# A linear attention and gated MLP kernel: the spatial products of one more batch in quarters, and a new written order

## The chip, the cores and the metric

One Trainium2 chip, one NeuronCore of it. The metric is the device time of one execution in microseconds (us), the median of the runs shown. The engines are named as in the profile: PE (TensorE) multiplies matrices, PEld is its loading of weights, DVE (VectorE), ACT (ScalarE) and POOL (GpSimd) work element by element, SP (SyncE) issues the DMAs. PE writes into PSUM, the rest lies in SBUF.

## What is computed

```python
f = 1.0 / (1.0 + np.exp(-f_logit))                  # q, k, v, f_logit: [4, 8, 768, 48]
for t in range(S):                                  # forgetting linear attention
    state = f[:, :, t, :, None] * state + np.einsum('bhd,bhe->bhde', k[:, :, t], v[:, :, t])
    y[:, :, t] = np.einsum('bhd,bhde->bhe', q[:, :, t], state)
x = y.transpose(0, 2, 1, 3).reshape(4, 768, 384)
h = np.maximum(x @ w_in, 0.0)                       # w_in [384, 1024]
u, v = (h[..., :d_ff // 2], h[..., d_ff // 2:])     # 512 columns each
v_n = (v - mu) / np.sqrt(var + 1e-06)               # layer norm of each row of v
v_s = np.einsum('ts,bsd->btd', w_spatial, v_n) + b_spatial[None, :, None]   # w_spatial [768, 768]
out = (u * v_s) @ w_out                             # w_out [512, 384]
```

Products are made in three passes: each operand is split into a high part (fp32r) and the low rest, and high x high, high x low and low x high are summed in PSUM.

## The kernel before

**A written order.** `PLAN` (line 46) is a list of steps; `run` calls `step_<name>` with the numbers behind the colon. Within `tc.manual_schedule()` each engine does its instructions in the order of that list, so an instruction that waits holds up all that stands behind it on its engine. `BESIDES` (line 114) names the steps that go to POOL in place of their usual engine. Buffers are `Slots`: `take` gives the buffer that has been free longest, `done` gives it back after the stated number of uses, and so the order of the plan also says whose buffer each step inherits.

**Attention.** 24 units (4 batches x 6 blocks of 128 rows, number n), each a chain of small steps: c, e, z, h, g, k, q and fm prepare forget factors, keys and queries (DVE, ACT, POOL; fm copies the last factors into `ends`), X are the scores on PE (L384), w, m, kv, YS, Yq, r0 to r2 the rest, ys copies the result, xt transposes it on PE into an `mm` bank, and xh (ACT) and xl (DVE) take it out of there as high and low part of `xT`.

**The MLP**, b = batch, th = half of the rows: V:b,u (nine products of 512 columns, L493) with vr, bs, na, nb, nc, vn (layer norm) and vh, vl (high and low part, buffers `vns`, six pairs); U:b,th,c (nine of 384, L584) with ur; S:b,th,c, the spatial product (18 of 384, L598) with sg (DVE, adds the bias); sm multiplies with u (POOL, L614); sh, sl split; O:b,th,tt (twelve of 384, L629; the last three in a part Oa and a part O) with oc (copy) and od (store). PSUM is `mm`, four single banks of 512 columns for V, U, S, O and the transposes, and `bp`, two pairs of them for the attention.

**Batch 3 in quarters.** Batches 0 to 2 make v_s of eight S steps a batch. Batch 3 takes the 2 x 2 blocks of w_spatial and v_n and makes seven block products in place of eight (Strassen's way, in Winograd's form). The block sums of w_spatial come from the steps LR:i (a load on SP of two of its row blocks into a buffer of `raws`), ra:i (four subtractions that depend on each other), th, tl, rh, rl (split into `low_b`, `out_b`, `cross_b`; rl:i gives the raw buffer back). Those of v_n, some of them in the vr buffers themselves, come from vd, dh, dl, sa (three instructions that depend on each other), zh, zl, yh, yl. The products are P:k,m (L779), k = 1 to 7 and m = 0, 1, nine of 384 columns each; xa to xg (DVE, L793) add them out of PSUM. "more" and "fast" hand over buffers of finished stages to `raws`, `vrs`, `uTs` and `gts`, "fast" after the last attention unit.

**The flag.** marks, check and load count the forget factors that underflow; hint (L839) lets PE load the flag and announces the jump at L885 to its sequencer, 45 products ahead of the end. The jump's target, which does everything again in another way, isn't entered with these inputs.

Of the kernel before, what the change touches and what calls it, by code (L numbers as in the profile page):

```python
# [40 lines left out]
LAST_C = 1  # L41
SUMMED = 6
# [61 lines left out]
    zh:2 xc:0 P:4,0 xc:1 P:4,1 zh:0 xb:1 zl:0 sa:1 O:2,1,2 zh:1 yh:2 zl:1 O:2,1,0 xb:0 sm:3,0,0 zl:2 check load P:6,1
    yh:1 oc:2,1,2 od:2,1,2 yh:0 sm:3,0,1 yl:1 ur:3,1,0 xd:1 sh:3,0,1 P:6,0 O:2,1,1 xd:0 sh:3,0,0 yl:2 yl:0 xe:1 xe:0
    P:5,0 sm:3,0,2 sm:3,0,3 sh:3,0,3 U:3,1,3 xf:0 P:3,0 sm:3,1,2 sh:3,0,2 sl:3,0,2 sl:3,0,1 sl:3,0,3 sh:3,1,2 oc:2,1,1
    od:2,1,1 oc:2,1,0 od:2,1,0 sl:3,0,0 P:5,1 ur:3,1,3 xg:0 sm:3,1,0 O:3,0,1 oc:3,0,1 od:3,0,1 xf:1 sm:3,1,3 O:3,0,0
    oc:3,0,0 od:3,0,0 O:3,0,2 oc:3,0,2 od:3,0,2 P:3,1 hint U:3,1,1 sh:3,1,0 sl:3,1,0 sh:3,1,3 ur:3,1,1 sl:3,1,2 xg:1
    sl:3,1,3 sm:3,1,1 Oa:3,1,0 sh:3,1,1 Oa:3,1,2 sl:3,1,1 O:3,1,0 oc:3,1,0 od:3,1,0 O:3,1,2 Oa:3,1,1 oc:3,1,2 od:3,1,2
    O:3,1,1 oc:3,1,1 od:3,1,1  # L110
# [4 lines left out]
    c:1 c:3 r2:0 c:5 r2:2 c:6 r2:3 c:7 c:9 c:8 r2:6 c:10 r2:7 r2:8 c:13 r2:10 r2:12 c:16 c:17 r2:14 c:19 r2:16 c:20  # L115
    r2:18 c:22 r2:19 r2:21 q:23 ra:1 r2:22 vd:1 vn:3,5
# [26 lines left out]
def tile_kernel(ctx, tc, fkq, fn, vv, w_cv, w_spT, b_sp, out):  # L143
# [524 lines left out]
    def step_fast():  # L668
# [9 lines left out]
        for slots, more in ((uTs, tiles(pool, "uT_fast", 2, [P, TH])), (vrs, tiles(pool, "vr_fast", 2, [P, G])), (gts, tiles(pool, "gt_fast", 2, [P, TH]))):  # L678
# [8 lines left out]
    def low_b(i):  # L687
        return [x[:, i] for x in xTs.of("t1")]
# [35 lines left out]
    def step_vd(i):  # L724
        x = vrs.of((B - 1, i))
        other("vd", i, nc.vector).tensor_tensor(x[:, right], x[:, left], x[:, right], op=ALU.subtract)

    def step_dh(i):
        nc.scalar.copy(vns.of((B - 1, i))[0][:, right], vrs.of((B - 1, i))[:, right])

    def step_dl(i):
        (hi, lo), x = vns.of((B - 1, i)), vrs.of((B - 1, i))
        nc.vector.tensor_tensor(lo[:, right], x[:, right], hi[:, right].bitcast(F32), op=ALU.subtract)

    def step_sa(i):

        x, y = vrs.of((B - 1, i)), vrs.of((B - 1, HK + i))
        eng = other("sa", i, nc.vector)
# [4 lines left out]
    def step_zh(i):  # L743
        high_of(vns.take(("z", i), 4), vrs.of((B - 1, HK + i)))

    def step_zl(i):
        low_of(vns.of(("z", i)), vrs.of((B - 1, HK + i)))
        vrs.done((B - 1, HK + i))

    def low_sum(i):  # L750
# [258 lines left out]
```

## Time and profile before

| | |
|---|---|
| median of the 3 runs shown | 348.38 us (348.37 to 349.01) |
| the profiled execution | 347.48 us |
| its span | 345.9 us |
| DMA | 38.48 MB |

The span runs from the first to the last instruction or transfer in the trace; the rest of an execution lies around it. A row of the trace has a start and a duration; since the engines are pipelined, an instruction may start a little ahead of the former's end. In a group of waits, "A <- B" reads: A's engine sat idle until B ended.

### The profile page before, as it was taken

How to read it: one execution, taken by the hardware profiler on the slowest of the kernel's cores; microseconds unless marked ns; L12 is line 12 of the kernel's file. 1: busy time of each engine (PE TensorE's matmuls, PEld its weight loads, DVE VectorE, ACT ScalarE, POOL GpSimd, SP SyncE). 2: the span in 40 equal slices, each digit the busy share in tenths (PEclk: the TensorE clock that was granted, in tenths of full speed). 3: DMA queues.
4: the chain of work that ended last, by engine and by line, in shares of the span. 5: the costliest groups of instructions: out<-in, count | busy, mean ns of one | idle time of the engine just before them, and what ended most of it. 6: DMA issues, size and time to landing. Idle time of an engine off the chain costs nothing.

```text
span 345.9 us, 10531 instructions
## 1 busy us (share of the span) xinstructions
PE 334.6 (97%) x4571; PEld 308.7 (89%) x4571; DVE 230.8 (67%) x445; ACT 181.0 (52%) x373; POOL 88.0 (25%) x103
## 2 busy tenths in 40 slices
PE   7888999999999999999999999999999999999995
PEld 5666788998999989899999889999999999999995
DVE  2898999985989898762755585662221796975420
ACT  7577898956457467732274356652222635522232
POOL 3215505302320061311603051007111125002500
PEclk9999999999999999999999999999999999999999
DMA  7989665151454221350330206210230031000112
GB/s 240 341 262 355 226 219 215 18 195 55 176 156 171 94 82 64 132 161 16 101 115 24 93 25 229 72 49 0 52 134 2 0 114 48 0 0 25 45 71 75
DMA packets 15508, 38.48 MB, mean 111 GB/s; under 512 B 1504, under 2 KB 9952, under 8 KB 15456
## 3 DMA queue, kind: packets, MB, share of 16 engines
q1 hardware_dynamic: 15456, 37.75, 32.0%
q8 instruction: 37, 0.61, 0.8%
q14 instruction: 15, 0.12, 0.1%
HBM read 33.03 MB, written 4.72 MB: 109 GB/s over the span
## 4 chain that ended last, share of the span: by engine, by line
PE 85%; DVE 6%; DMA 3%; ACT 2%; issue 2%; POOL 0%; SPq 0%; DVEq 0%; ACTq 0%
PE mm L598 22%; PE mm L629 14%; PE mm L584 13%; PE mm L493 13%; PE bp L779 6%; PE bp L384 5%; PE bp L436 3%; PE bp L448 3%; PE bp L408 2%; PE mm L460 2%; DMA fkq<-fn 2%; DMA late<-w_spT 1%; DVE fkq L356 1%; PE mm L339 1%; PE mm L779 1%
## 5 line engine op out<-in xcount | busy, mean ns | idle before, releaser
L614 POOL TENSOR_TENSOR uT<-gt,uT 128x384 f32<-128x384 f32 x24 | 26.8, 1126 | 53.9 <-DVE gt L607 23.8
L324 POOL TENSOR_SCALAR fkq<-fkq 112x512 f32<-112x512 f32 (+1 forms) x14 | 21.8, 1555 | 43.6 <-DMA fkq<-fkq 17.7
L427 POOL TENSOR_TENSOR sA<-sA,F 112x192 f32<-112x192 f32 x14 | 9.7, 691 | 80.1 <-DVE sA L422 79.7
L598 PE MATMUL mm<-w_sph,vnh 128*128 128x384 f32 x144 | 29.9, 342 | 0.0
L598 PE MATMUL mm<-w_sph,vnl 128*128 128x384 f32 x144 | 29.2, 338 | 0.0
L598 PE MATMUL mm<-w_spl,vnh 128*128 128x384 f32 x144 | 29.2, 338 | 0.0
L646 ACT COPY osb<-mm 128x384 f32<-128x384 f32 x24 | 11.1, 481 | 28.7 <-PE mm L629 27.0
L598 PEld LDWEIGHTS mm<-w_spl,vnh 128*128 128x128 f32 x144 | 25.6, 188 | 0.0
L598 PEld LDWEIGHTS mm<-w_sph,vnl 128*128 128x128 f32 x144 | 25.6, 188 | 0.0
L598 PEld LDWEIGHTS mm<-w_sph,vnh 128*128 128x128 f32 x144 | 25.2, 188 | 0.4
L607 DVE TENSOR_TENSOR gt<-mm,b_bc 128x384 f32<-128x384 f32 x23 | 12.7, 551 | 18.9 <-PE mm L598 18.8
L384 PE MATMUL bp<-q,fkq 48*64 48x112 f32 x768 | 23.9, 261 | 1.1 <-issue 0.4
L475 DVE TENSOR_TENSOR xTl<-mm,xTh 128x384 fp32r<-128x384 f32 x24 | 13.3, 552 | 16.0 <-ACT xTh L470 15.9
L356 DVE SCALAR_TENSOR_TENSOR fkq<-fkq 112x512 f32<-112x512 f32 x24 | 18.2, 757 | 8.5 <-ACT fkq L350 4.7
L334 DVE TENSOR_TENSOR_SCAN fkq<-runs,fkq 112x512 f32<-112x512 f32 x18 | 22.9, 1277 | 0.7 <-ACT fkq L329 0.6
L584 PE MATMUL mm<-xTh,w_inh 128*128 128x384 f32 x96 | 22.8, 346 | 0.0
L384 PEld LDWEIGHTS bp<-q,fkq 48*64 48x64 f32 x768 | 19.0, 133 | 3.9 <-issue 1.7
L584 PE MATMUL mm<-xTl,w_inh 128*128 128x384 f32 x96 | 22.1, 338 | 0.0
L584 PE MATMUL mm<-xTh,w_inl 128*128 128x384 f32 x96 | 22.1, 338 | 0.0
L493 PE MATMUL mm<-w_inh,xTh 128*128 128x512 f32 x72 | 22.0, 413 | 0.0
L629 PE MATMUL mm<-w_outh,gh 128*128 128x384 f32 x96 | 21.8, 344 | 0.0
L622 DVE TENSOR_TENSOR gl<-uT,gh 128x384 fp32r<-128x384 f32 x27 | 15.1, 570 | 9.2 <-ACT gh L618 9.2
(210 smaller groups left out, 823.0 us busy)
## 6 DMA issues: line engine op xcount, KB each, us to landing
fkq<-fkq SPq DMA_DIRECT2D x18, 768.0 KB, 4.8
val<-vv SPq DMA_DIRECT2D x24, 192.0 KB, 4.5
out<-osb SPq DMA_DIRECT2D x24, 192.0 KB, 2.0
words<-w_cv SPq DMA_DIRECT2D x4, 768.0 KB, 7.9
fkq<-fkq SPq DMA_DIRECT2D x6, 512.0 KB, 5.5
late<-w_cv SPq DMA_DIRECT2D x2, 768.0 KB, 5.3
late<-w_spT SPq DMA_DIRECT2D x2, 768.0 KB, 6.1
fkq<-fn SPq DMA_DIRECT2D x6, 192.0 KB, 3.7
```

Of the source, the lines that this page charges most:

```text
L324: other("c", n, nc.vector).tensor_scalar(f, f, -LOGIT_MOST, None, op0=ALU.max)
L334: return nc.vector.tensor_tensor_scan(f[0:DP], runs, f[0:DP], 0.0, op0=ALU.mult, op1=ALU.add)
L356: other("k", n, nc.vector).scalar_tensor_tensor(k, f, 1.0 / F_LEAST, k, op0=ALU.min, op1=ALU.mult)
L384: nc.tensor.matmul(sc[to, e, cs], k[dr, at:at + C], qs[n % 2][dr, j, chunk], start=True, stop=True)
L475: nc.vector.tensor_tensor(x[1], mm.of(("xt", n))[:, 0:HD].rearrange("p (c t) -> p c t", c=KX), x[0].bitcast(F32), op=ALU.subtract)
L493: nc.tensor.matmul(acc, xs[:, c, ut * P:(ut + 1) * P], ws[:, c, G:FF], start=i == 0, stop=i == 3 * KX - 1)
L584: nc.tensor.matmul(acc[:, 0:TH], ws[:, kx, cs], xs[:, kx, :], start=i == 0, stop=i == 3 * KX - 1)
L598: nc.tensor.matmul(acc[:, 0:TH], vns.of((b, ks))[va][:, cs], w_sp_s[wb][:, ks, th * TH:(th + 1) * TH], start=i == 0, stop=i == 3 * KS - 1,)
L614: nc.gpsimd.tensor_tensor(uT, gts.of((b, th, c)), uT, op=ALU.mult)
L622: nc.vector.tensor_tensor(lo, uTs.of((b, th, c)), hi.bitcast(F32), op=ALU.subtract)
L629: nc.tensor.matmul(acc[:, 0:DM], gs.of((b, th, c))[ga][:, ts], w_out_s[wb][:, c, :], start=c == cs[0] != LAST_C and ga == wb == 0, stop=c ...
L779: nc.tensor.matmul(acc, vns.of(user(i))[va][:, cs], b(i)[wb], start=n == 0 and k in (1, 2, 7), stop=n == 3 * HK - 1, skip_group_check=True)
```

## The change

Batch 2 is made in quarters as well (`FAST = 2, 3`), so its eight S steps go and 14 P steps, P:2,k,m, come with the steps around them: vd, dh, dl, sa, zh, zl, yh, yl and xa to xg take the batch as a first number. Batch 2 needs the upper blocks of v_n again after their low parts are made; a new step rc (two additions, high + low) makes the values anew from the parts where the buffer was needed in between.

The whole plan from sl:0,0,0 on is in a new order. The loads of w_spatial's blocks come as LR:0, 2, 1, ra is on DVE for all of them, and the raw buffers go LR:0 <- "more", LR:2 <- "fast", LR:1 <- rl:0. `low_b` lies in a part of `w_sp` that nothing reads any more, and not in an `xT` buffer. "fast" hands over four vr and one uT in place of two and two. POOL gets sa, vd, rc, vn and q steps by the new `BESIDES`, and loses ra:1. hint stands 138 products ahead of the end.

```diff
+FAST = 2, 3
 PLAN:
-    V:3,4 bs:3,2 ur:2,1,1 th:1 tl:1 xh:23 xl:23 V:3,5 bs:3,1 ur:2,1,2 marks na:3,0 bs:3,3 vr:3,4 S:2,1,2 LR:2 sl:2,0,3
-    rh:1 vr:3,5 bs:3,4 S:2,1,3 od:1,1,1 rl:1 od:1,1,0 LR:0 bs:3,5 ra:2 nb:3,0 sg:2,1,2 sh:2,0,1 sl:2,0,1 na:3,1 nb:3,1
...
+    sl:1,1,3 r2:22 kv:23 r0:23 Yq:22 ys:22 V:3,1 vn:2,4 vl:2,3 r1:23 Yq:23 ur:2,0,3 rc:2,0 xh:21 xl:21 vh:2,4 xt:22
+    xh:22 ys:23 P:2,1,0 vl:2,4 ur:2,0,0 vr:3,1 xt:23 dh:2,2 tl:0 xh:23 fm:23 fast rh:0 LR:2 V:3,2 ra:2 vr:3,2 rl:0
+    U:2,1,1 fm:22 O:1,1,0 od:1,0,1 dl:2,2 rc:2,2 ur:2,1,1 xa:2,0 xl:23 P:2,2,0 sa:2,2 rh:2 P:2,1,1 th:2 oc:1,1,0
+    od:1,0,2 od:0,1,0 LR:1 O:1,1,1 tl:2 V:3,5 ra:1 rl:2 sa:2,0 xa:2,1 rh:1 marks th:1 tl:1 xl:22 rl:1 oc:1,1,1 od:1,1,1
+    O:1,1,2 rc:2,1 P:2,7,0 sa:2,1 P:2,7,1 bs:3,1 zh:2,2 zh:2,0 xc:2,0 P:2,4,0 zh:2,1 zl:2,2 P:2,2,1 oc:1,1,2 od:1,1,2
...
+    ur:2,1,0 O:2,0,0 U:3,0,0 vl:3,0 oc:2,0,0 od:2,0,0 vd:3,2 P:3,1,1 vd:3,0 vn:3,4 sm:2,1,3 sm:2,1,1 vn:3,3 ur:3,0,1
+    dh:3,1 vh:3,3 xg:2,0 vl:3,5 P:3,1,0 O:2,0,2 dl:3,1 vl:3,3 sm:2,1,0 xa:3,1 xa:3,0 dh:3,0 dh:3,2 vh:3,4 vl:3,4 sa:3,1
+    O:2,0,1 dl:3,0 dl:3,2 P:3,7,1 xc:3,1 oc:2,0,2 od:2,0,2 sm:2,1,2 sh:2,1,2 sh:2,1,3 P:3,7,0 sa:3,0 sl:2,1,2 sh:2,1,1
...
 BESIDES:
-    c:1 c:3 r2:0 c:5 r2:2 c:6 r2:3 c:7 c:9 c:8 r2:6 c:10 r2:7 r2:8 c:13 r2:10 r2:12 c:16 c:17 r2:14 c:19 r2:16 c:20
-    r2:18 c:22 r2:19 r2:21 q:23 ra:1 r2:22 vd:1 vn:3,5
+    c:1 c:3 r2:0 c:5 r2:2 c:6 r2:3 c:7 c:9 c:8 r2:6 c:10 r2:7 r2:8 c:13 r2:10 r2:12 c:16 r2:13 c:17 vn:1,5 q:16 vn:1,4
+    r2:15 q:17 c:18 c:19 r2:16 q:19 c:20 c:22 r2:19 vn:2,1 vd:2,1 vd:2,0 q:21 r2:20 r2:21 vd:2,2 vn:2,4 sa:2,2 sa:2,0
+    rc:2,1 sa:2,1 vn:3,0 vd:3,0 vn:3,3 sa:3,0 sa:3,2
...
 step_vh:
-        if b == B - 1:
+        if b in FAST:
             n = 2 * P if u < HK else G
-            return nc.scalar.copy(vns.take((b, u), 4)[0][:, 0:n], vrs.of((b, u))[:, 0:n])
+            return nc.scalar.copy(vns.take((b, u), 5 if b == FAST[0] else 4)[0][:, 0:n], vrs.of((b, u))[:, 0:n])
...
 low_b:
-        return [x[:, i] for x in xTs.of("t1")]
+        return [w[:, i, TH:S] for w in w_sp_s]
...
+    def step_rc(b, i):
+        for u in (i, HK + i):
+            hi, lo = (x.bitcast(F32) for x in vns.of((b, u)))
+            other("rc", (b, i), nc.vector).tensor_tensor(vrs.take((b, u)), hi, lo, op=ALU.add)
+            vns.done((b, u))
```

## Rows read from the trace of the kernel before

**Rows 1.** The page, part 1: engine, busy us, share of the span, instructions.

```profile
PE 334.6 (97%) x4571; PEld 308.7 (89%) x4571; DVE 230.8 (67%) x445; ACT 181.0 (52%) x373; POOL 88.0 (25%) x103
```

**Rows 2.** Busy time by stretch: length, PE, PEld, DVE, ACT, POOL, PEclk, DMA.

```profile
120.00:342.40 222.40, 221.86 (x2445) 210.63 (x2443) 130.62 (x265) 97.05 (x207) 55.54 (x56) 1.00 0.20 65
```

**Rows 3.** PE's waits from 120 us on: us in total, times, longest.

```profile
PE bp L779 <- DVE gt L793: 0.3, 1, 0.3
PE bp L384 <- DVE fkq L356: 0.2, 1, 0.2
```

**Rows 4.** The chain of work: start, us, engine, line; products of a step.

```profile
169.59 2.09 PE mm L629 x12
...
229.66 3.17 PE mm L598 x18
...
243.18 2.09 PE mm L493 x9
...
332.90 1.58 PE bp L779 x9
```

**Rows 5.** PE and ACT in order of time: start, us, what.

```profile
270.59 0.94 PE L493 MATMUL mm<-w_inh,xTh 128*128 128x512 f32 x3
270.87 0.48 ACT L470 CAST xTh<-mm 128x384 fp32r<-128x384 f32 x1
...
273.46 0.50 ACT L700 CAST t3h<-late 128x384 fp32r<-128x384 f32 x1
273.86 0.83 ACT L700 CAST qt2h<-late 128x768 fp32r<-128x768 f32 x1
```

**Rows 6.** DVE in order of time, in stretches without POOL.

```profile
279.08 0.56 DVE L697 TENSOR_TENSOR raw_fast<-raw_fast 128x384 f32<-128x384 f32 x1
...
295.66 0.54 DVE L703 TENSOR_TENSOR t3l<-raw_fast,t3h 128x384 fp32r<-128x384 f32 x1
296.13 0.94 DVE L703 TENSOR_TENSOR qt2l<-raw_fast,qt2h 128x768 fp32r<-128x768 f32 x1
```

**Rows 7.** POOL in order of time: a vd, a q and a vn step.

```profile
235.93 1.28 POOL L360 TENSOR_TENSOR q<-fkq,F 112x512 f32<-112x512 f32 x1
...
282.79 0.98 POOL L726 TENSOR_TENSOR vr<-vr 128x256 f32<-128x256 f32 x1 [1.34 <-DVE vr L552]
...
287.60 2.62 POOL L552 TENSOR_SCALAR vr_fast<-vr_fast,mv,rs 128x512 f32<-128x512 f32 x1 [3.83 <-issue]
```

**Rows 8.** DVE and POOL in order of time, where both are at work.

```profile
35.06 0.96 DVE L260 SCALAR_TENSOR_TENSOR words<-words 128x768 int32<-128x768 int32 x1
36.04 0.51 POOL L427 TENSOR_TENSOR sA<-sA,F 112x192 f32<-112x192 f32 x1
36.06 1.31 DVE L261 SCALAR_TENSOR_TENSOR words<-words 128x768 int32<-128x768 int32 x1
...
41.58 1.61 POOL L369 COPY ends<-F 112x4 f32<-112x4 f32 x1
...
124.22 0.99 DVE L356 SCALAR_TENSOR_TENSOR fkq<-fkq 112x512 f32<-112x512 f32 x1
...
315.54 0.95 DVE L703 TENSOR_TENSOR vnl<-vr,vnh 128x256 fp32r<-128x256 f32 x1 [1.01 <-ACT vnh L700]
...
322.56 1.01 POOL L614 TENSOR_TENSOR uT<-gt,uT 128x384 f32<-128x384 f32 x1 [0.56 <-DVE gt L793]
323.06 0.92 DVE L622 TENSOR_TENSOR gl<-uT,gh 128x384 fp32r<-128x384 f32 x1 [0.59 <-ACT gh L618]
```

**Rows 9.** Instructions of the flag's load and of the jump on PE's queue.

```profile
L839 PEldq TENSOR_LOAD <-bad x1: 490/490/490, 331.2 to 331.2; - x1
...
L885 PEldq COMPARE_BRANCH  x1: 393/393/393, 339.1 to 339.1; - x1
```

**Rows 10.** DMA issues, 274 to 285 and 245 to 256 us: KB, us to landing.

```profile
late<-w_spT SPq DMA_DIRECT2D x1, 768.0 KB, 4.9
...
raw_fast<-w_spT SPq DMA_DIRECT2D x1, 768.0 KB, 5.6
```

More of the change, by code (lines that the diff above doesn't have):

```diff
@@ L104 @@
[L104 to L108, printed above, removed]
@@ new lines @@
+    yl:3,0 yh:3,1 zl:3,2 zl:3,1 zl:3,0 load P:3,6,0 sm:3,0,0 O:2,1,2 O:2,1,1 yl:3,2 yl:3,1 xd:3,0 P:3,5,0 sl:3,0,1 hint
+    P:3,6,1 xd:3,1 O:2,1,0 ur:3,0,3 oc:2,1,2 od:2,1,2 xe:3,0 xf:3,0 sm:3,0,2 xe:3,1 sh:3,0,0 sm:3,0,3 oc:2,1,1 od:2,1,1
+    sl:3,0,0 P:3,3,0 xg:3,0 sh:3,0,2 P:3,5,1 sh:3,0,3 sl:3,0,3 sm:3,1,0 sl:3,0,2 U:3,1,2 O:3,0,1 oc:3,0,1 od:3,0,1
+    O:3,0,2 ur:3,1,2 oc:3,0,2 od:3,0,2 sm:3,1,2 xf:3,1 oc:2,1,0 od:2,1,0 sm:3,1,3 sh:3,1,2 O:3,0,0 sh:3,1,3 oc:3,0,0
+    od:3,0,0 sl:3,1,3 P:3,3,1 sh:3,1,0 sl:3,1,0 xg:3,1 U:3,1,1 ur:3,1,1 sl:3,1,2 Oa:3,1,1 sm:3,1,1 Oa:3,1,2 sh:3,1,1
@@ L676, in pair @@
             return [tuple(pool.tile([P, width], F32R, name=f"{name}{k}{i}") for k in "hl") for i in range(HK)]
-        for slots, more in ((uTs, tiles(pool, "uT_fast", 2, [P, TH])), (vrs, tiles(pool, "vr_fast", 2, [P, G])), (gts, tiles(pool, "gt_fast", 2, [P, TH]))):
+        for slots, more in ((uTs, tiles(pool, "uT_fast", 1, [P, TH])), (vrs, tiles(pool, "vr_fast", 4, [P, G])), (gts, tiles(pool, "gt_fast", 2, [P, TH]))):
             slots.free.extend(more)
@@ L705, in step_th @@
     def step_th(i):
-        if "t1" not in xTs.held:
-            xTs.take("t1", 2)
         high_of(low_b(i), raws.of(i)[:, 0, 0:TH])
@@ L722, in tile_kernel, with step_vd, right_of, step_dh @@
     left, right = slice(0, W2), slice(W2, G)
[L724 to L738, printed above, removed]
+    def step_vd(b, i):
+        x = vrs.of((b, i))
+        other("vd", (b, i), nc.vector).tensor_tensor(x[:, right], x[:, left], x[:, right], op=ALU.subtract)
+    def right_of(user):
+        return [x[:, right] for x in vns.of(user)]
+    def step_dh(b, i):
+        high_of(right_of((b, i)), vrs.of((b, i))[:, right])
+    def step_dl(b, i):
+        low_of(right_of((b, i)), vrs.of((b, i))[:, right])
+        if b == FAST[0]:
+            vrs.done((b, i))
+    def step_rc(b, i):
[3 more added lines that the diff above has]
+            vns.done((b, u))
+    def step_sa(b, i):
+        x, y = vrs.of((b, i)), vrs.of((b, HK + i))
+        eng = other("sa", (b, i), nc.vector)
         eng.tensor_tensor(y[:, right], y[:, right], x[:, right], op=ALU.subtract)
@@ L741, in step_sa, with step_zh, step_zl, low_sum @@
         eng.tensor_tensor(y[:, left], y[:, left], y[:, right], op=ALU.subtract)
[L743 to L750, printed above, removed]
-        return [x[:, left] for x in vns.of(("y", i))]
-    def step_yh(i):
-        vns.take(("y", i), 2)
-        high_of(low_sum(i), vrs.of((B - 1, i))[:, left])
-    def step_yl(i):
-        low_of(low_sum(i), vrs.of((B - 1, i))[:, left])
-        vrs.done((B - 1, i))
-    def step_P(k, m):
+    def step_zh(b, i):
+        high_of(vns.take(("z", b, i), 4), vrs.of((b, HK + i)))
+    def step_zl(b, i):
+        low_of(vns.of(("z", b, i)), vrs.of((b, HK + i)))
+        vrs.done((b, HK + i))
+    def low_sum(b, i):
+        return [x[:, left] for x in vns.of(("y", b, i))]
+    def step_yh(b, i):
+        vns.take(("y", b, i), 2)
+        high_of(low_sum(b, i), vrs.of((b, i))[:, left])
+    def step_yl(b, i):
+        low_of(low_sum(b, i), vrs.of((b, i))[:, left])
+        vrs.done((b, i))
+    def step_P(b, k, m):
         L, R = slice(m * P, (m + 1) * P), slice(W2 + m * P, W2 + (m + 1) * P)
@@ L779, in step_P @@
                 nc.tensor.matmul(
-                    acc, vns.of(user(i))[va][:, cs], b(i)[wb], start=n == 0 and k in (1, 2, 7), stop=n == 3 * HK - 1, skip_group_check=True
+                    acc, vns.of(user(i))[va][:, cs], w(i)[wb], start=n == 0 and k in (1, 2, 7), stop=n == 3 * HK - 1, skip_group_check=True
                 )
@@ L784, in step_P @@
             vns.done(user(i))
-        if k == 5:
-            xTs.done("t1")
     def bias(th):
@@ L936, in tile_kernel @@
             xf = again.tile([P, KX, TH], F32, name="xf")
+            nc.gpsimd.dma_start(xf, w_spT[0:HK * P, TH:S].rearrange("(k p) n -> p k n", p=P))
+            nc.scalar.copy(w_sp_s[0][:, 0:HK, TH:S], xf)
+            nc.vector.tensor_tensor(w_sp_s[1][:, 0:HK, TH:S], xf, w_sp_s[0][:, 0:HK, TH:S].bitcast(F32), op=ALU.subtract)
             with tc.For_i(0, B) as b:
```

124 lines of the change are left out of this document (62 added, 62 removed).

## The prediction

> **What bounds the kernel now.** First the page's share of each engine: PE is busy 97% of the span, against 67% for DVE [rows 1]. PE's share is a mean over a start that waits for data and a rest that doesn't, so the second view is the busy time by stretch: from 120 us to PE's last product at 342.4, PE is busy 221.86 of 222.40 us, DVE 130.62 and POOL 55.54, at a granted clock of 1.00, the higher of PE's two levels (2.4 GHz) [rows 2]. The plan is the same up to the step sl:0,0,0; what the change reorders begins at about 120 us of the trace, so it lies within this stretch, in which PE leaves 0.54 us idle. The third view, who PE waited for from 120 us on, names two waits of 0.3 and 0.2 us, both ended by DVE [rows 3]. So in the changed part time goes with the number of products, as long as PE finds its operands ready; a gain there is real, and it is lost only where PE has to wait.
>
> **What the products give.** In the chain of work an S step (18 products of 384 columns) takes 3.17 us and a P step (9 of them) 1.58 [rows 4]. Batch 2's spatial product was 8 S steps, 8 x 18 = 144 products; it becomes 14 P steps, 14 x 9 = 126. The 18 saved are one S step: **-3.17 us**. All other steps of PE are the same ones in another order. The tail is the same too: six long and three short O steps as Oa and O, one copy, one store, 3.5 us from PE's last product to the end of the span [rows 2].
>
> **What is added to the other engines.** ACT: three dh, yh and zh more, nine copies of 256 and 512 columns at about 0.5 us, for 384 take 0.50 [rows 5]: some 4.5 us. DVE: sums out of PSUM, low parts, rc:2,0 and rc:2,2, less what goes to POOL: about 4 us net by 0.56 for 384 columns [rows 6]. POOL: fifteen instructions of sa and three more vd at 0.98, two of rc and three more q at 1.28, five more vn at 2.62 and one c, less the four of ra:1 at 1.01 [rows 7, 8]: 17.6 + 6.4 + 13.1 + 1 to 2 - 4.0, **34 us more**, from 55.5 to some 90. As sums all of this lies beside PE and costs nothing; the question is where it stands right in front of a product.
>
> **The jump.** PE's own load of the flag took 0.49 us at 331.2, and PE's products ran on through it, because the sequencer stands ahead of them [rows 2, 9]. Moved 93 products forward it finds the same lead: 0. Without that lead it would cost its 0.49. The jump itself (0.39 us at 339.1) is done 2.9 us ahead of PE's last end at 342.4 [rows 9], so what an earlier announcement may win or lose is hidden up to that.
>
> **The tight place: O:1,1,2.** I followed the products of the new order back to the steps that must come before each, with the durations of the rows. Most have a slack of 0.5 us and more. One has none. O:1,1,2 takes the PSUM bank that xt:22 held, free only after xl:22; xl:22 stands on DVE behind ra:1, rl:2, xa:2,1, marks and tl:1; ra:1 needs the load LR:1; and LR:1 goes into the buffer that rl:0 frees. I count from the start of V:3,2, the product behind xt:23. **PE's way** to O:1,1,2 is V, U, O, P, P, O, V: 2.09 + 1.58 + 2.09 + 1.58 + 1.58 + 2.09 + 2.09 = 13.1 us (U has nine products as wide as P's) [rows 4]. **The other way**: xh:23 starts 0.28 behind that V's start, lasts 0.48, and the copies of rh:0 follow, the second 0.40 behind the first and 0.83 long: 1.9 by the starts, each 0.08 ahead of the former's end [rows 5]; rl:0's second subtraction 0.95, to 2.9; LR:1 goes out at once and lands after 4.9 us, as the last of these loads did, or 5.6, as the one beside two stores [rows 10]: 7.8 to 8.5. ra:1 is four instructions that depend on each other, 2.2; rl:2 1.34 (0.54 and 0.94, each handing on 0.07 ahead of its end); xa:2,1, tl:1 and xl:22 0.47 to 0.56 each, and marks, three small ones, taken as one more: together 1.95 [rows 6]. Sum 13.3 to 14.0. PE waits **0.2 to 0.9 us** if nothing disturbs DVE; I take 0.5, as one store may be on its way. On SP only stores are queued behind LR:1, so its waiting harms nobody; LR:0 and LR:2 come 10 us and 2 us early by the same count.
>
> **But POOL disturbs it.** From about 4.6 us on this count POOL has sa:2,2, sa:2,0, rc:2,1 and sa:2,1 in its queue, eleven instructions with two SBUF operands, some 9 us without a break, and ra:1, rl:2 and tl:1 on DVE read two SBUF operands as well. The trace shows what such a pair does: a DVE subtraction that began at 323.06 inside a POOL product (322.56 to 323.57) ended 0.41 us after that, 0.92 us long where one of 384 columns takes 0.54 [rows 6]. The other way round, a POOL copy of four columns took 1.61 us at 41.58, through DVE subtractions written one behind the other [rows 8]. Each collision costs what is left of one POOL instruction, 0.35 us in the mean for a product of 256 columns (about 0.7 long, between 0.51 for 192 and 1.01 for 384). DVE meets one at ra:1's first instruction and, since xa:2,1 reads PSUM and lets POOL in, perhaps one before tl:1: **0 to +0.8**; I take 0.5. So the wait at O:1,1,2 is 1.0 us.
> The Trainium skill states it as a rule (SBUF — State Buffer, "Who interferes with whom"): the port pair that DVE and GpSimd share is an exclusive lock, whoever issues first keeps it for the whole instruction and the other is fully blocked. The rows at 323.06 and 41.58 agree; by the rule the wait is 1.0 us, with a shared and unlocked port it would be 0.5.
>
> **The waits elsewhere.** Both waits of the kernel before have a POOL product in their cause: the DVE step k:14 ran 0.99 us inside one, and PE's X behind it waited; the subtraction at 315.54 took 0.95 inside one, for 256 columns as long as one of 768 at 296.13, and the sums behind it kept PE [rows 3, 6, 8]. With 90 us of POOL for 55, 0.5 us becomes 0.8: **+0.3**. Bounds: -0.5 if all are gone, +1.3 if X:23 (half a microsecond of slack, with vd:2,2 and vn:2,4 on POOL beside its chain) meets two POOL products.
>
> **Sum.** -3.17 + 1.0 + 0.3 = -1.9. The profiled execution took 347.48 us, its span 345.9 and 1.6 around it, and becomes 345.6; the median of the runs shown is 348.38, 0.9 above it, and becomes **346.5**.
>
> **Rivals.** *POOL and DVE take turns (slower).* ra:1's instructions depend on each other, and between such DVE leaves some hundredths of a microsecond. At 36.04 a POOL product that was waiting went in by just such a gap, and the dependent DVE instruction at 36.06 took 1.31 us, 0.35 more than its like before it; the blocked copy of 1.61 stood behind independent ones [rows 8]. If POOL enters every gap of ra:1, it brings two sa instructions of 0.7 and one of rc at 1.3 in between, 2.7, and 0.3 more before tl:1: with 0.5 from the load the wait is 3.5 us, up to 4.2. -3.17 + 3.5 + 0.5 elsewhere = +0.8, **349.2** (348.3 to 350.4). It decides from a wait of 2.9 us at O:1,1,2 on. For it speaks the row at 36.04, against it that it is one row, and that POOL needs its queue full just then. *DVE is not disturbed.* The load lands after 4.9 us and POOL's queue comes at another time: wait 0.2, and elsewhere -0.3, as one of the two old waits goes: **345.1**. *A second place.* P:3,7,1 needs dl:3,2, which stands on DVE behind vl:3,4 and sa:3,1 and beside sa:3,2 on POOL; its slack is some 1 us, and three POOL products in between, of 0.7 each, use it up and 1.2 more: **347.7**.
>
> **Chances.** Forecast 0.38, taking turns 0.36, undisturbed 0.14, second place 0.12. A measurement of this kernel can tell about 0.2%, 0.7 us, from no change. Faster by more than that: nearly all of the forecast and of the undisturbed case, half of the second place, a little of the turns: 0.59. Within it: two fifths of the turns, half of the second place: 0.22. Slower: the rest of the turns, 0.19. Range: from the undisturbed case to the turns' upper part, **345.0 to 350.0**; the forecast's own, by its bounds, is 345.2 to 347.6.
>
> **What would show it.** 18 products fewer on PE, and P steps of 1.58 us. PE's idle time from 120 us on grows from 0.5 to about 1.3 us, the largest wait in front of an O step, with DVE's xl as its releaser. ra:1 starts on DVE 4.9 to 5.6 us behind rl:0's end; its four instructions take 2.2 to 2.6 us if I am right, and about 5 if they take turns with POOL. PE's row around the announcement has no gap. I am wrong if PE waits in front of the first P steps of either batch, if the tail of 3.5 us changes, or if PE's busy time falls by other than 3.2 us.

## The result: 353.83 us, 1.3% slower

The median is 353.83 us (352.1 to 357.67, six runs) against 348.57 for the kernel before in the same session: a ratio of 1.0134, with a 95% interval of 1.0108 to 1.0159. The longest of the six, 357.67 us at a mean granted clock of 0.979, is the profiled one, and the ratio leaves it out. On another chip it was 355.05 against 349.21, 1.0164 (1.0133 to 1.0195). The forecast was 346.5, its range ended at 350.

The profile after, the page's part 1, to be set beside [rows 1]:

```profile
PE 335.9 (94%) x4553; PEld 310.4 (87%) x4553; DVE 249.1 (70%) x453; ACT 182.7 (51%) x382; POOL 121.6 (34%) x128
```

The 18 products are gone (4571 to 4553) and POOL has 34 us more, as counted; yet PE is busy for longer, and its share is lower. The stretch that the change reorders begins with the product step V:1,3 and ends with PE's last product. Busy time in this stretch, kernel before and changed kernel (stretch, length, PE, PEld, DVE, ACT, POOL, PEclk, DMA, as in [rows 2]):

```profile
116.53:342.37 225.84, 225.33 (x2463) 213.70 (x2461) 133.67 (x270) 98.73 (x210) 55.54 (x56) 1.00 0.20 66
```

```profile
119.80:350.47 230.67, 224.87 (x2445) 213.22 (x2442) 152.28 (x278) 100.53 (x219) 88.39 (x80) 0.99 0.20 65
```

The profiled execution's span is 356.1 us, 10.2 more than before, and these two rows split it. The stretch begins 3.3 us later, which isn't the change: between 14 and 40 us the granted clock was 0.87 in this execution, and in some executions of kernels with and without the change it falls there (below). The stretch itself is 4.8 us longer, and 5.6 us lie behind it in place of 3.5. DVE is busy for 18.6 us more in the stretch, where about 4 were counted; with every form of instruction at the lower quartile of its durations in these two traces the growth is 4.3, and the rest is instructions that took longer than usual. From here on I count from V:1,3 on: 229.4 us to the end before, 236.3 after, 235.4 in another execution of the changed kernel.

What PE waited for in the changed kernel, against 0.3 and 0.2 us in [rows 3]:

```profile
PE mm L636 <- DVE xTl L480: 3.8, 1, 3.8
PE mm L498 <- ACT uT L596: 1.6, 1, 1.6
PE bp L389 <- DVE fkq L361: 0.4, 1, 0.4
```

The first is O:1,1,2 behind xl:22, the tight place of the prediction, with 3.8 us in place of 1.0. The chain of work shows how that O step and the three P steps behind it ran:

```profile
256.62 4.21 PE mm L636 x12
260.83 5.56 PE bp L796 x27
```

An O step takes 2.09 in [rows 4] and three P steps 4.7. The same stretch in the view of busy time by stretch: PE's wait, these steps, what follows.

```profile
252.80:256.60 3.80, 0.01 (x1) 0.00 (x0) 3.77 (x9) 0.30 (x1) 2.80 (x3) 0.89 0.14 52
256.60:263.00 6.40, 6.38 (x21) 6.38 (x22) 2.08 (x4) 0.00 (x0) 0.00 (x0) 0.53 0.00 0
263.00:268.00 5.00, 5.00 (x31) 5.00 (x30) 3.39 (x7) 2.92 (x6) 0.38 (x1) 1.00 0.21 77
```

Behind the wait the granted clock is 0.53, nearly all of it at the lower level (1.2 GHz), and 1.00 again from 263 us on.

Last the jump, to be set beside [rows 9], and PE's end in the chain:

```profile
L900 PEldq COMPARE_BRANCH  x1: 4072/4072/4072, 347.1 to 347.1; - x1
```

```profile
344.10 6.37 PE mm L636 x36
350.47 0.03 ACTq L653
```

On PE's queue it takes 4.07 us where it took 0.39. It begins at 347.1, 3.4 us ahead of the end of PE's last product, and ends at 351.2, 0.7 us behind it. The span doesn't end with the jump: it ends 1.06 to 1.07 us behind the landing of the last store, in both kernels and in every profiled execution of the experiments. From that store's issue on (342.9 before, 351.0 in the changed kernel) the view of the DMA issues has

```profile
out<-osb SPq DMA_DIRECT2D x1, 192.0 KB, 1.9
```

before and

```profile
q8 instruction: 1, 0.02, 2.2%
out<-osb SPq DMA_DIRECT2D x1, 192.0 KB, 4.0
```

after, and these 2.1 us are what the tail grew by. In both traces a 16 KB transfer of instructions (queue q8) begins 0.7 us behind the end of the jump. Before, it runs from 340.19 to 341.62 us and is over when the store is issued. In the changed kernel it runs from 351.94 to 353.72, inside the store, and the store's last nine packets move from 353.70 on. That the transfer holds the store up is read from these times; no experiment takes the one away and leaves the other.

### The profile page after: what moved, and what is told of

It is laid out like the page before. It is cut to its first block, busy times and chain, and to the rows that moved or that the text cites. A ratio compares the mean times of both kernels' runs of the same rounds, so it can differ in the third digit from the quotient of the medians.

```text
span 356.1 us, 10542 instructions
## 1 busy us (share of the span) xinstructions
PE 335.9 (94%) x4553; PEld 310.4 (87%) x4553; DVE 249.1 (70%) x453; ACT 182.7 (51%) x382; POOL 121.6 (34%) x128
## 4 chain that ended last, share of the span: by engine, by line
PE 77%; DVE 8%; DMA 7%; ACT 2%; POOL 2%; issue 1%; SPq 1%; DVEq 0%; ACTq 0%; POOLq 0%
PE mm L605 14%; PE mm L636 13%; PE mm L591 13%; PE mm L498 11%; PE bp L796 10%; DMA fkq<-fkq 6%; PE bp L389 5%; PE bp L441 3%; PE bp L453 3%; PE bp L413 2%; PE mm L465 2%; PE mm L796 1%; DMA late<-w_spT 1%; DVE q L365 1%; DVE sc L399 1%
## 5 line engine op out<-in xcount | busy, mean ns | idle before, releaser
L329 POOL TENSOR_SCALAR fkq<-fkq 112x512 f32<-112x512 f32 (+1 forms) x15 | 25.8, 1723 | 35.9 <-DMA fkq<-fkq 21.1
L629 DVE TENSOR_TENSOR gl<-uT,gh 128x384 fp32r<-128x384 f32 x30 | 18.3, 615 | 11.0 <-ACT gh L625 10.9
L596 ACT ACTIVATE uT<-mm 128x384 f32<-128x384 f32 x30 | 14.7, 493 | 15.4 <-PE mm L591 10.2
L636 PE MATMUL mm<-w_outh,gl 128*128 128x384 f32 x96 | 21.8, 345 | 0.0
L636 PE MATMUL mm<-w_outl,gh 128*128 128x384 f32 x96 | 21.8, 345 | 0.0
L636 PEld LDWEIGHTS mm<-w_outh,gh 128*128 128x128 f32 x96 | 17.2, 193 | 4.4 <-DVE xTl L480 4.2
L498 PE MATMUL mm<-w_inh,xTl 128*128 128x512 f32 x72 | 20.7, 395 | 0.0
L498 PE MATMUL mm<-w_inl,xTh 128*128 128x512 f32 x72 | 20.7, 395 | 0.0
L441 PEld LDWEIGHTS bp<-val,sc 64*64 64x64 f32 x768 | 13.9, 137 | 7.3 <-issue 3.4
L625 ACT CAST gh<-uT 128x384 fp32r<-128x384 f32 x30 | 15.0, 513 | 9.9 <-PE mm L636 5.7
```

Of the source, the lines that this page charges most:

```text
L329: other("c", n, nc.vector).tensor_scalar(f, f, -LOGIT_MOST, None, op0=ALU.max)
L441: nc.tensor.matmul(y[to, e, cs], s[rows, keys[e]], v[rows, hd], start=j == 0, stop=False, skip_group_check=True)
L498: nc.tensor.matmul(acc, xs[:, c, ut * P:(ut + 1) * P], ws[:, c, G:FF], start=i == 0, stop=i == 3 * KX - 1)
L629: nc.vector.tensor_tensor(lo, uTs.of((b, th, c)), hi.bitcast(F32), op=ALU.subtract)
L636: nc.tensor.matmul(acc[:, 0:DM], gs.of((b, th, c))[ga][:, ts], w_out_s[wb][:, c, :], start=c == cs[0] != LAST_C and ga == wb == 0, stop=c ...
```

## The experiments

"The rest" is the time from V:1,3 to the end of the span in each profiled execution; "tail" is what of it lies behind PE's last product. Ratios are to the kernel before on the same chip.

| kernel | us | ratio (95%) | rest | tail | jump |
|---|---|---|---|---|---|
| before | 348.57 | 1 | 229.4 | 3.5 | 0.39 |
| changed | 353.83 | 1.0134 (1.0108 to 1.0159) | 236.3 | 5.6 | 4.07 |
| changed, again | 355.05 | 1.0164 (1.0133 to 1.0195) | 235.4 | 5.6 | 4.08 |
| xl:22 first | 349.41 | 1.0009 (0.9989 to 1.0029) | 230.3 | 5.1 | 3.98 |
| PE filled | 351.87 | 1.0080 (1.0051 to 1.0110) | 232.0 | 3.9 | 0.39 |
| POOL quiet | 349.24 | 1.0014 (0.9987 to 1.0041) | 228.9 | 4.4 | 3.32 |

**The changed kernel again.**

> The changed kernel again, on the same chip as the next three. What is to be told apart: in its first profiled execution PE's granted clock also fell twice between 20 and 32 us, in the part that is the same in both kernels, and the reordered part began 3.2 us late. Theory A (that dip is a property of some executions and no part of the change): another execution has a clock of 1.00 up to 120 us, the dip behind the wait at O:1,1,2 remains, and the time is 352 to 354 us. Theory B (the change also slows the start): the dip between 20 and 32 us is there again and the time is above 355 us.

The wait of 3.8 us, that of 1.6 and the tail of 5.6 were there again; the time was 355.05 us, and between 20 and 40 us the clock was 0.91. So the signs of theory B came, the time only just. Its claim doesn't follow: of the runs below, the changed kernel with the announcement at 45 or without it has a clock of 1.00 between 14 and 40 us, the kernel before without the announcement 0.87. What brings the dip about is open; no reading here rests on it.

**xl:22 ahead of ra:1.**

```diff
-    V:3,5 ra:1 rl:2 sa:2,0 xa:2,1 rh:1 marks th:1 tl:1 xl:22 rl:1
+    V:3,5 xl:22 ra:1 rl:2 sa:2,0 xa:2,1 rh:1 marks th:1 tl:1 rl:1
```

> Only xl:22 is moved on DVE, from behind tl:1 to in front of ra:1. Theory A (O:1,1,2 waits for the bank of xt:22 and for nothing else, and the slower products behind it follow from that wait): no wait at O:1,1,2; P:2,7,0 waits some 1.1 us for the low part of the load LR:1, whose chain is as slow as before; the granted clock stays at 1.00 in 240 to 280 us; time 5 to 6 us under the changed kernel's, 348 us. Theory B (O:1,1,2 waits for something else beside): its wait of 3.8 us stays within 1 us and so does the time.

PE's waits:

```profile
PE mm L498 <- ACT uT L596: 1.6, 1, 1.6
PE bp L796 <- DVE t3l L710: 1.0, 1, 1.0
PE bp L389 <- DVE fkq L361: 0.4, 1, 0.4
```

No wait at O:1,1,2; P:2,7,0 waits 1.0 us for the late chain in its place (1.1 expected), and the clock stays at 1.00 behind it (252 to 260 us). The time is 5.6 us less than the changed kernel's on the same chip. So that one position of a 0.5 us instruction on DVE was worth 5.6 us, of which the wait itself is 2.8. Busy time from V:1,3 to PE's last product, in this run and in the changed kernel again:

```profile
119.01:344.21 225.20, 222.17 (x2445) 210.50 (x2443) 151.90 (x278) 100.44 (x219) 87.95 (x80) 1.00 0.20 67
```

```profile
118.33:348.06 229.73, 223.69 (x2445) 212.05 (x2443) 152.00 (x278) 100.53 (x219) 88.54 (x80) 0.99 0.20 65
```

**PE kept busy through the wait.**

```diff
-    tl:2 V:3,5 ra:1
+    tl:2 V:3,5 fill:21 ra:1
+    def step_fill(count):
+        for _ in range(count):
+            nc.tensor.matmul(fast_bank(FAST[0], 0, 1), vns.of((FAST[0], 0))[0][:, 0:P], w_sp_s[0][:, 0, 0:TH], start=True, stop=True, skip_group_check=True)
```

> 21 extra products of 384 columns (3.7 us) behind V:3,5, into a PSUM bank that nothing else uses at that time; nothing is moved. They fill the time in which PE waits for xl:22. Theory A (the products behind the wait run at half the clock because PE stood idle in front of them): the granted clock is 1.00 there, O:1,1,2 takes 2.1 us in place of 4.2, the P step behind it 1.6, and the time is 2.9 us under the changed kernel's, 350.5 to 351, though PE does more work. Theory B (these products are slow for what they read or for what else runs then): they stay slow and the time is the same within 0.5 us.

```profile
252.00:256.00 4.00, 3.83 (x22) 3.51 (x21) 3.97 (x9) 0.00 (x0) 2.45 (x3) 1.00 0.13 49
256.00:260.00 4.00, 4.00 (x25) 4.00 (x24) 2.07 (x4) 0.00 (x0) 0.00 (x0) 1.00 0.00 0
```

The clock stays at 1.00 and O:1,1,2 begins as late as before but runs at full speed: the slow products come from PE's idle time and not from what they read. The price of the fall is the busy time that the same 2445 products took beyond that in the run with xl:22 first (222.17 us, clock 1.00): 224.87 - 222.17 = 2.7 us in the first execution and 223.69 - 222.17 = 1.5 in the second. Of the 3.2 us that this kernel won on the same chip, the other 1.7 are the tail's: it has 3.9 and a jump of 0.39 us, which nobody had expected of it. That led to the runs on the jump further down.

**POOL quiet beside ra:1.**

```diff
-    ra:1 rl:2 sa:2,0 xa:2,1 rh:1 marks th:1 tl:1 xl:22 rl:1 oc:1,1,1 od:1,1,1 O:1,1,2 rc:2,1 P:2,7,0 sa:2,1
+    ra:1 rl:2 xa:2,1 rh:1 marks th:1 tl:1 xl:22 rl:1 oc:1,1,1 od:1,1,1 O:1,1,2 sa:2,0 rc:2,1 P:2,7,0 sa:2,1
 BESIDES:
-    sa:2,2 sa:2,0 rc:2,1 sa:2,1 vn:3,0
+    sa:2,2 vn:3,0
```

> sa:2,0, rc:2,1 and sa:2,1 go from POOL to DVE, behind rl:1, so that POOL has only sa:2,2 in its queue when ra:1 begins. Theory A (POOL and DVE took turns): ra:1's four instructions take 2.2 to 2.4 us in place of 4.4, rl:2 1.3 in place of 3.0, xl:22 ends some 0.1 us before V:3,5 does, the wait at O:1,1,2 is under 0.5 us and the clock stays at 1.00; time 6 to 7 us under the changed kernel's, 347 us. Theory B (the load LR:1 or the length of DVE's own queue made the wait): ra:1 takes over 4 us still, or the wait stays above 2 us.

DVE and POOL in order of time in the changed kernel (start, us; L701 to L704 are ra:1, L710 rl:2, L754 to L756 sa:2,0 and sa:2,1, L747 rc:2,1):

```profile
247.02 0.82 DVE L701 TENSOR_TENSOR late<-late 128x384 f32<-128x384 f32 x1 [0.89 <-DMA late<-w_spT]
247.51 0.94 POOL L755 TENSOR_TENSOR late<-vr,late 128x256 f32<-128x256 f32 x1
247.88 0.98 DVE L702 TENSOR_TENSOR late<-late 128x384 f32<-128x384 f32 x1
248.40 1.05 POOL L756 TENSOR_TENSOR vr<-vr 128x256 f32<-128x256 f32 x1
248.89 0.98 DVE L703 TENSOR_TENSOR late<-late 128x384 f32<-128x384 f32 x1
249.42 1.61 POOL L747 TENSOR_TENSOR vr_fast<-vnh,vnl 128x512 f32<-128x512 f32 x1
249.90 1.54 DVE L704 TENSOR_TENSOR late<-late 128x384 f32<-128x384 f32 x1
250.99 1.61 POOL L747 TENSOR_TENSOR vr<-vnh,vnl 128x512 f32<-128x512 f32 x1
251.37 1.65 DVE L710 TENSOR_TENSOR t3l<-raw_fast,t3h 128x384 fp32r<-128x384 f32 x1
252.68 0.92 POOL L754 TENSOR_TENSOR vr<-vr,vr_fast 128x256 f32<-128x256 f32 x1
252.94 1.48 DVE L710 TENSOR_TENSOR qt2l<-raw_fast,qt2h 128x768 fp32r<-128x768 f32 x1
```

and DVE in the kernel with POOL quiet (L699 to L702 are ra:1, L708 rl:2):

```profile
245.70 0.56 DVE L699 TENSOR_TENSOR late<-late 128x384 f32<-128x384 f32 x1 [0.47 <-DMA late<-w_spT]
246.29 0.56 DVE L700 TENSOR_TENSOR late<-late 128x384 f32<-128x384 f32 x1
246.89 0.56 DVE L701 TENSOR_TENSOR late<-late 128x384 f32<-128x384 f32 x1
247.48 0.56 DVE L702 TENSOR_TENSOR late<-late 128x384 f32<-128x384 f32 x1
247.96 0.55 DVE L708 TENSOR_TENSOR t3l<-raw_fast,t3h 128x384 fp32r<-128x384 f32 x1
248.43 0.95 DVE L708 TENSOR_TENSOR qt2l<-raw_fast,qt2h 128x768 fp32r<-128x768 f32 x1
```

The first list is to be read as a zip: from the second on, each DVE instruction of 384 columns ends 0.4 us behind the end of POOL's (the one of 768 columns 0.8), and each POOL instruction ends 0.6 us (256 columns) or 1.2 us (512 columns) behind the end of DVE's. ra:1 takes 4.4 us, alone 2.3; rl:2 2.97, alone 1.3. The Trainium skill (SBUF — State Buffer, "Who interferes with whom") calls the port pair that the two engines share an exclusive lock, for which a DVE instruction with two SBUF inputs contends with a GpSimd instruction that reads SBUF. The trace agrees: these instructions have two SBUF inputs, and behind an rc addition of 512 columns a DVE subtraction of 384 takes 1.54 to 1.65 us in place of 0.56. With POOL quiet the wait at O:1,1,2 is gone though DVE has eight instructions more to do, and the rest is 228.9 us, 0.4 less than before though the tail is 0.9 longer. The time is 349.24 us, no faster than the kernel before; 347 were expected.

**The announcement back at 45 products, or left out, in the changed kernel.**

```diff
-    P:3,5,0 sl:3,0,1 hint P:3,6,1
+    P:3,5,0 sl:3,0,1 P:3,6,1
...
-    xg:3,1 U:3,1,1
+    xg:3,1 hint U:3,1,1
```

> The changed kernel with the announcement of the jump back at 45 products ahead of the end, where the kernel before has it; all else as changed. In the changed kernel the jump takes 4.07 us on PE's queue (0.39 before) and the span goes on for 5.6 us behind PE's last product (3.5 before). Theory A (announced 138 products ahead, the jump has lost its head start by the time it comes): the jump takes 0.39 us again, the span ends 3.5 to 3.9 us behind PE's last product, time some 1.8 us under the changed kernel's 353.8 to 355. Theory B (the place of the announcement doesn't matter, but where the code of the end lies, which 21 extra products had shifted): the jump takes 3.3 us or more still, the time is the same within 0.5 us.

> The changed kernel without the announcement; the load of the flag stays where it is. Theory A (in the changed kernel the announcement comes too early and is as good as none): the jump takes about 4 us as with it, and the time is the same within 0.5 us. Theory B (the announcement does some of its work also 138 products ahead): the jump is longer than 4.1 us and the time is some 0.5 us or more above the changed kernel's.

The jump took 4.04 and 3.59 us, the times were 354.44 (1.0164, 1.0120 to 1.0207) and 354.62 (1.0174, 1.0128 to 1.0219), as without these edits as far as these intervals can tell. The announcement doesn't make the jump fast in the changed kernel, wherever it stands: the first theory, that it comes too early, falls. With POOL quiet and the announcement at 45:

> The kernel with sa:2,0, rc:2,1 and sa:2,1 on DVE, with the announcement at 45 products. There the jump took 3.3 us and the span went on for 4.4 us behind PE's last product. Theory A: jump 0.39 us, 3.5 to 3.9 us behind the last product, time 0.6 to 0.9 us less than with the announcement at 138, 348.5 us. Theory B: no difference above 0.3 us.

349.6 us (1.0002, 0.9974 to 1.0029), jump 3.54: no difference either.

**q:21 on DVE.** The wait of 1.6 us in front of V:2,4 has a POOL instruction in its cause again (changed kernel):

```profile
205.37 1.28 POOL L365 TENSOR_TENSOR q<-fkq,F 112x512 f32<-112x512 f32 x1 [0.76 <-ACT F L350]
205.43 1.64 DVE L629 TENSOR_TENSOR gl<-uT,gh 128x384 fp32r<-128x384 f32 x1
207.10 0.49 ACT L596 ACTIVATE uT<-mm 128x384 f32<-128x384 f32 x1 [1.80 <-DVE gl L629]
```

> As the kernel with the announcement at 45 and POOL quiet, and q:21 on DVE in place of POOL. In the changed kernel sl:1,0,2 on DVE took 1.57 us inside q:21 on POOL, ur:1,1,1 waited for it, and a V step for that, 1.6 us. Theory A (the wait comes from that collision): the V step's wait is 0.6 us or less though DVE has 0.7 us more to do, time 1.0 to 1.6 us under that of the kernel with q:21 on POOL, 347 us, 1.5 to 2 us under the kernel before. Theory B (DVE is late there by its own work): the wait stays above 1.2 us and the time is the same.

```profile
PE bp L794 <- DVE gt L806: 0.6, 1, 0.6
PE mm L496 <- ACT uT L594: 0.5, 1, 0.5
PE bp L387 <- DVE fkq L359: 0.4, 1, 0.4
```

1.6 became 0.5, and the time 348.2 us, 0.9970 (0.9944 to 0.9996): the first version ahead of the kernel before, with a tail of 5.6 us still (347 were expected).

**Where the jump stands.** Six runs on the number of PE's products ahead of the jump and on the announcement, in both kernels. With 18 idle products more at the start (D:10 in front of Yq:0, D:5 in front of Yq:1, D:6 for D:3), the last version and the changed kernel:

> As the kernel with POOL quiet, q:21 on DVE and the announcement at 45, with 18 more of the idle products on a buffer of zeros in the first 25 us (ten in front of Yq:0, five in front of Yq:1, three more in D:3), where PE waits for 1.2 and 0.6 us anyway. PE then has as many products ahead of the jump as in the kernel before. Theory A (the jump is slow or fast by where the end lies in PE's sequence of instructions, which the 18 saved products moved): the jump takes 0.39 us, the span ends 3.5 to 3.9 us behind the last product in place of 5.6, time 1.5 to 2.1 us less, 346 to 346.7. Theory B (it is something else in the changed kernel): the jump takes over 3 us still.

> The changed kernel with the same 18 idle products at the start and nothing else; the announcement stays 138 products ahead. Theory A (the end's place in PE's sequence of instructions): the jump takes 0.39 us, the span ends 3.5 to 3.9 us behind the last product, time 1.5 to 2.1 us under the changed kernel's. Theory B: as before these products, within 0.5 us.

The kernel before with 18 less (D:11 for D:29), without the announcement, without it and one product more, with nine products less:

> The kernel before with 18 of its idle products at the start left out (D:29 becomes D:11), so that PE has as few products ahead of the jump as the changed kernel. Theory A: the jump takes 3.3 to 4.1 us and the span ends 4.4 to 5.6 us behind the last product (3.5 with them): 1 to 2 us slower than the kernel before, as far as the start takes the same time. Theory B (something else in the changed kernel): jump 0.39 us, tail 3.5.

> The kernel before without the announcement, the load of the flag in its place. Theory A (by the place of the end in the sequence, the announcement changes nothing): jump 0.39 us, same time within 0.3 us. Theory B (the announcement is what makes the jump fast there): the jump takes 3.5 us or more, the span ends some 2 us later.

> The kernel before without the announcement, as in the earlier run (jump 3.67 us), with one more idle product at the start (D:30), so that the jump stands one instruction further in PE's sequence than in the kernel before and not one nearer. Theory A (the announcement itself makes the jump fast, where it works): the jump is slow, over 3.3 us. Theory B (that run was slow because leaving out the announcement moved the jump by one instruction): 0.39 us.

> The kernel before with nine of its idle products less (D:20), half of the way to the changed kernel's place of the jump. Where between the two places does the jump turn slow? Both theories leave it open; it takes either 0.39 us or 3.3 us and more, and nothing in between if it is a matter of the place alone.

The row of the jump in the kernel before with 18 less and with nine less:

```profile
L885 PEldq COMPARE_BRANCH  x1: 3682/3682/3682, 342.8 to 342.8; - x1
```

```profile
L885 PEldq COMPARE_BRANCH  x1: 482/482/482, 339.2 to 339.2; - x1
```

By the number of products on PE (the run with 4562 of the changed kind is the last one below):

| products | announced | jump, us (program) | tail, us |
|---|---|---|---|
| 4553 | 138 or 45 ahead | 3.32 to 4.08 (changed, seven executions), 3.68 (before) | 4.4 to 5.6, 4.6 |
| 4553 | no | 3.59 (changed) | 4.4 |
| 4562 | 45 ahead | 0.48 (before), 0.49 (changed) | 3.5, 3.7 |
| 4571, 4574 | 138 or 45 ahead | 0.39 (before), 0.39 to 0.40 (changed) | 3.5 to 3.9 |
| 4571, 4572 | no | 3.67, 3.35 (before) | 5.0, 4.7 |

The jump is fast when it is announced and when 4562 to 4574 products stand in PE's sequence; how far ahead it is announced changes nothing. One without the other gives 3.3 to 4.1 us, in either program. The tail goes with it: the last store lands 1.8 to 2.2 us behind its issue in the eight executions with a fast jump and 2.8 to 4.0 in the eleven with a slow one. In the eight the transfer of instructions behind the jump is over before that store is issued. In ten of the eleven the store's last nine packets begin within 0.03 us of that transfer's end, also in the kernel before without the announcement and with one product more, where the jump itself ends with PE's last product.

As times: the kernel before with 18 products less took 350.86 us (1.0057, 1.0029 to 1.0086), without the announcement 350.52 (1.0060, 1.0036 to 1.0084) and 349.8 (1.0035, 1.0006 to 1.0064, one product more), with nine less 348.3 (0.9978, 0.9944 to 1.0012). In the first two the start has a part in this, for V:1,3 begins at 119.8 and 120.0 us there; from V:1,3 on the three slow ones took 230.9, 230.9 and 230.5 us against 229.4. The two with idle products at the start show the jump of 0.39 and tails of 3.9 and 3.8, but little gain in time (348.13, 0.9985; 354.15, 1.0162): their V:1,3 begins at 119.2 and 119.3 us, though the clock was 1.00 in both, so I had put these products where they cost some 2 us.

**Without idle products.** The instructions can come from products cut in two.

```diff
+                halves = (slice(0, TH // 2), slice(TH // 2, TH)) if (b, k) == (2, 6) else (slice(0, TH),)
+                for h in halves:
+                    nc.tensor.matmul(acc[:, h], vns.of(user(i))[va][:, cs], w(i)[wb][:, h], start=n == 0 and k in (1, 2, 7), stop=n == 3 * HK - 1, skip_group_check=True)
```

> The kernel with POOL quiet, q:21 on DVE and the announcement at 45, with the 18 products of P:2,6,0 and P:2,6,1 made in two halves of 192 columns each: as many columns, 36 more instructions ahead of the jump, and nothing in the first 25 us. Theory A (the jump is fast by its place in PE's sequence): the jump takes 0.39 us, the span ends 3.5 to 3.9 us behind PE's last product in place of 5.6, both P steps take 1.58 us still, time 1.3 to 2 us under the kernel without the halves, 346.5 to 347, and 1.5 to 2.5 us under the kernel before. Theory B: jump over 3 us, same time.

> The changed kernel with the same two P steps in halves, nothing else. Theory A: jump 0.39 us with the announcement 138 products ahead, the span ends 3.5 to 3.9 us behind the last product, time 1.3 to 2 us under the changed kernel's 354 to 355 (5.8 us over the kernel before on the same chip becomes 4 to 4.5). Theory B: no gain above 0.5 us.

Both have a jump of 0.40 us, and tails of 3.7 and 3.9. The halves aren't free: the two P steps together take 4.0 us in place of 3.2, and PE is busy 1.0 us longer (223.15 against 222.17). The changed kernel with them took 354.05 (1.0110, 1.0054 to 1.0166): against the changed kernel again a gain of 0.9 us by the medians and 1.9 by the ratios, not clear of none; in its profiled execution the slow clock behind the wait cost 2.5 us (225.65 busy against 223.15). The quiet version with them took 347.55, 0.9956 (0.9930 to 0.9982): half a microsecond better than without them, where 1.3 to 2 were expected. With one P step in halves, and bs:3,1 behind xc:2,0 on DVE:

> The fastest kernel so far with two edits: only P:2,6,0 in halves (P:2,6,0 and P:2,6,1 in halves had cost 1.0 us of PE time), which puts the jump where the kernel before with nine products less has it (0.48 us there), and bs:3,1 behind xc:2,0 on DVE, since PE's P:2,4,0 waited 0.4 us for xc:2,0 behind it. Theory A: jump 0.4 to 0.5 us, span 3.5 to 3.9 us behind the last product, PE 0.5 us less busy and 0.4 us less idle, time 0.5 to 1 us under the kernel with 18 halved products, 346.5 to 347, some 2 to 2.5 us under the kernel before. Theory B (at this place the announcement works only in the other program): jump over 3 us, no gain.

```profile
L901 PEldq COMPARE_BRANCH  x1: 487/487/487, 339.1 to 339.1; - x1
```

346.87 us, **0.9928 (0.9902 to 0.9954)**: the change with these two POOL collisions and the slow jump taken out is 2.4 us faster than the kernel before. Against the changed kernel this version has five edits: sa:2,0, rc:2,1 and sa:2,1 on DVE behind rl:1, q:21 on DVE, the announcement at 45, nine products in halves, bs:3,1 later.

## Why the prediction was wrong

The sum went by three terms: products, the wait at O:1,1,2, waits elsewhere. Two of the three were too small, the jump and the tail were put at 0, and the clock behind a wait wasn't priced. In the first execution, from V:1,3 on: products -3.2, idle time +5.3 (5.8 against 0.5), clock +2.7, tail +2.1, together +6.9; in the second -3.2 + 5.5 + 1.5 + 2.1 = +6.0. The medians differ by 5.3 and 5.8.

- *Products, -3.17:* right. At a clock of 1.00 the two rows of PE's busy time, 225.33 and 222.17, differ by 3.16.
- *O:1,1,2:* the place, its mechanism and the load were right, the term was mis-sized: 1.0 predicted, 3.8 measured. LR:1 landed 7.6 us behind V:3,2's start (7.8 to 8.5 predicted). From there to xl:22's end I had 2.2 + 1.34 + 1.95 and it took 4.4 + 3.0 + 2.2. The step that failed is "Each collision costs what is left of one POOL instruction": I counted one or two of them. In fact all six instructions of ra:1 and rl:2 met one, and these two steps took 3.9 us more than I had put down for them. The rival of the turns had wait (3.5, up to 4.2) and reason right, its signs came (a wait over 2.9 us, ra:1 at 4.4 where it said about 5), and I gave it 0.36. I held the row at 41.58 against it, where a POOL copy seemed to be kept out by independent DVE instructions. But rl:2's two subtractions, which don't depend on each other, alternated with POOL as well: a queue of POOL instructions is enough.
- *What a wait costs:* the forecast and the rivals priced a wait at its length. Behind 3.8 us without work PE's clock was at its lower level, and that cost 1.5 to 2.7 us more. The trace of before could hardly show it, for from 120 us on PE waits 0.3 us there at most.
- *The jump, 0:* wrong. "It finds the same lead" was said of the load of the flag, and that holds (0.49 us at 322.9, no gap on PE). But the jump itself became ten times as long. It still ends only 0.7 us behind PE's last product; what it moves is the transfer of instructions behind it, into the time of the last store, which lands 2.1 us later. I had called the tail the same, and had made it a sign of my error if it changed; I hadn't looked for what else the number of PE's instructions could move.
- *Waits elsewhere, +0.3:* the size short: 1.6 at V:2,4 and 0.4 at X:23, less the 0.5 of before. The cause was right for V:2,4 (a POOL product under a DVE step on the way to PE; with q:21 moved, 1.1 of the 1.6 went), but the place wasn't foreseen: I had counted it among those with slack. X:23 was the place that I had named for the upper bound; its wait is in the first execution and not in the second, which has 0.6 in front of an L441 product in its place. P:3,7,1 had no wait.
- *The rival's 349.2* with the tail's 2.1 and the clock's 1.5 to 2.7 added is 352.8 to 354.0: even the right story, as I priced it, ended 4.6 us short of 353.83.

## What to carry to other kernels

Where POOL has a queue of two-operand work, count a DVE chain with two SBUF inputs beside it as alternating with it, each of its instructions longer by one of POOL's (here 0.4 to 1.1 us), and take such work off POOL before taking anything else; a slack of half a microsecond is none. Price a wait of PE of several microseconds with the slower clock behind it, and let a short instruction that frees a PSUM bank go ahead of a chain that waits for a transfer. After any edit that changes the number of PE's instructions look at the row of the last jump, at the landing of the last store and at the tail: a saving in the middle can be lost at the end, and a few instructions more can win it back.

## What the hardware showed beyond that

An announced jump takes 0.39 to 0.49 us with 4562, 4571 or 4574 products in the program and 3.3 to 4.1 with 4553, in two programs with different orders. Where between 4553 and 4562 it turns, whether it turns back elsewhere, and by what, the runs leave open. Behind the jump's end a 16 KB transfer of instructions begins, 0.7 to 0.8 us later in 17 of the 19 executions, and where it falls into the last store, that store lands 2.8 to 4.0 us behind its issue in place of 1.8 to 2.2. The granted clock fell behind a wait of 3.8 us, and not behind waits of 1.6 us (1.00 from 200 to 236 us in the changed kernel) or of 1.0. Two products of 192 columns took longer than one of 384: the two P steps in halves 4.0 us in place of 3.2.
